# Gated mix of linear attention and a GEGLU MLP on one core: x blocks by position, wide sums and splits, phi into a zeroed tile, key sums by group

## The chip, the cores and the metric

The kernel runs on one core of a Trainium2 chip. The metric is device time in microseconds (us) of one execution, and of several executions the median. Beside those, one execution was taken with the hardware profiler; all rows of the profile and the trace come from that one.

The engines by their names in the profile: PE is TensorE's matmul, PEld its weight load, DVE is VectorE, ACT is ScalarE, POOL is GpSimd, SP is SyncE. In this kernel SP and POOL compute nothing: they issue DMAs. A "q" behind an engine's name stands for its sequencer.

## The reference

With S = 2048 tokens, D = 1024, H = 32 heads of 32 and a hidden width of 3584:

```python
g = sigmoid((x * gate_w).sum(-1, keepdims=True))
a = A(x, wqkv, w_phi, wo)          # linear attention
b = B(x, w_gate, w_up, w_down)     # (gelu(x @ w_gate) * (x @ w_up)) @ w_down
return g * a + (1 - g) * b

# A:
q, k, v = split(x @ wqkv)          # 32 heads of 32
pq, pk = q @ w_phi, k @ w_phi      # per head
phi_q = concat([softmax(pq), softmax(-pq)])      # 64 features, the same for phi_k
kv = phi_k^T @ v;  z = phi_k.sum(over tokens)
o = (phi_q @ kv) / (phi_q @ z + 1e-6)
a = o @ wo
```

Everything is float32.

## The kernel before

**Products.** Each large product is a block scheme with seven products in place of eight (Strassen's): x is cut into 2 x 2 blocks by token half and feature half (positions 11, 12, 21, 22), and four sums of these blocks, with three plain blocks, are the operands `x10, s1, s2, x11, s3, s4, x01`. For float32 accuracy each operand is split in two float32r parts, an upper one that ScalarE makes by a copy (`high`, L56) and a lower one that VectorE makes by a subtraction (`low`, L59). A product of 4 chunks of 128 is 12 matmuls of 128x512: upper by upper, upper by lower, lower by upper (`PASSES`), so the weights' lower half is asked for first by the third matmul.

**Units.** The work before the output part is a list of units: 8 of values (`v`), 8 of keys (`k`), then for each token half query units (`q`) and 28 gate and up units (`g`, `u`). A unit is seven slots of 12 matmuls on TensorE (L768); a slot takes some 2.72 us. `weights(n, ...)` loads a unit's weight block in even and odd part (`e`, `o` in "stage" tiles), splits e as `x`, forms sums of e and o (`quarter_sums`, `more_sums`), and splits these as `y` and `z` in tiles of the tag "tyz" (three buffers, `slot()`). `results(n, ...)` takes the products out of PSUM: L786, L800, L815 and L817 are ScalarE's copies between banks (the banks are a, b, c, c11, p), L781 is VectorE's subtraction of two products into a tile of the tag "h" (`hidden()`, three buffers).

**Order.** The order on TensorE, VectorE, ScalarE and SP is written at build time. Work that belongs to no fixed place is a Python generator (a "stream"): each `yield lo, hi, d, a` says from which slot on it may go, by which slot it must, and its costs on VectorE and ScalarE in us. `run_slot` takes streams that fit in the slot, by an estimate of both engines' clocks, and those that are due. Every engine then runs its list strictly in order: an instruction that waits holds all behind it.

**The start.** Values need x itself as weights and wv as moving data. `raws[i]` is a tile with the four positions of chunk pair i (three in "tyz" buffers, the fourth in three "h" buffers and one "qx"). A loop over the 8 chunks splits what has come and runs 12 matmuls each; `w_steps` makes the four sums in place, one chunk of 512 columns at a time (`sum_steps`), spread over this loop and units 1 and 2 by the table `extra`. `sums_high` and `sums_low` split them, 512 columns at a time. `phi_c` is loaded by one DMA and multiplied with a block mask into `bps`, the block diagonal weights with which `fold_piece` and others fold w_phi into wk and wq (L304, L447).

**Value stores.** `split_values` (L164 to L168) splits a result and stores it to DRAM in tensor `vt`, through buffers given by `value_homes` in turn: one "qx" buffer and three quarters of a work tile (`gated`).

**Features.** For each key half, group of four heads (8 groups) and 512 tokens there is a job (32 in all): max and min, exponentials, sums, scaled features f; f is added by an accumulating POOL DMA to `z_sum[g]` in DRAM (L985); then f is split and multiplied with the values (L1001), and `finish_kv` adds the result to `kz`. Jobs of key half 1 come first, then those of half 0, group by group.

**finish_z and attention.** After all of these, `finish_z` loads the eight `z_sum[g]` of 128x1024 in turn, reduces each over tokens (L1058), brings the sums into order, stores them in `z_rows` and spreads them by eight POOL DMAs into `kz` (L1081). `attention` then runs 32 jobs: `front` loads a query block (L1087), transposes it (L1106) and subtracts max and min; then come exponentials (L1138), the denominator with the sums z that `load_sums` has brought (L1092), the scaling, a transpose, the split (`pts`), and four matmuls (`attend`, L1205) whose results are stored for the output part. The output part (L1468) follows the last unit.

Of the kernel before, what the change touches and what calls it, by code (L numbers as in the profile page):

```python
# [16 lines left out]
P = 128  # L17
# [16 lines left out]
def tile_gated_mix(ctx: ExitStack, tc: tile.TileContext, x, xT, wkT, wqT, wv, w_phi, wo,  # L34
# [151 lines left out]
    with tc.manual_schedule(engines={PE, DVE, ACT, SP}):  # L186
# [5 lines left out]
        mask = fp.tile([P, 4, 32], F32, tag="st", name="mask", bufs=1)  # L192
        nc.vector.memset(mask, 0.0)
        for j in range(4):
            nc.vector.memset(mask[32 * j:32 * j + 32, j, :], 1.0)

        x_ops = {}
        raws = []
        for i in range(4):
            if i < 3:  # L200
                t = mid.tile([P, 4, BLK], F32, tag="tyz", name="raw", bufs=3)
                raws.append([t[:, n] for n in range(4)])
            else:
                raws.append([hidden() for _ in range(3)] + [fp.tile([P, BLK], F32, tag="qx", name="raw", bufs=1)])
# [13 lines left out]
        phi_c = fa.tile([P, NG, 32], F32, tag="o2", name="phi_c", bufs=1)  # L218
        nc.gpsimd.dma_start(phi_c, w_phi.rearrange("(g h) d f -> (h d) g f", h=4))
# [25 lines left out]
        x_sums = [w_steps(*raws[i]) for i in range(4)]  # L245
        ready = []

        steps_done = [0] * 4

        def sum_steps(n, upto=4):  # L250
            while n:
                left = [i for i in ready if steps_done[i] < upto]
                if not left:
                    break
                i = min(left, key=lambda i: (i > 0 and steps_done[i], i))
                next(x_sums[i])
                steps_done[i] += 1
                n -= 1

        bps = []  # L260
        for s in range(KC):
# [13 lines left out]
            if s >= 2:  # L275
                sum_steps(1)
            if s % 2:
                ready.append(i)
            if s == 3:
                both = fp.tile([P, 2, 4, 4, 32], F32, tag="vs", name="bp", bufs=1)  # L280
                for h in range(2):
                    t = both[:, h]
                    nc.vector.tensor_tensor(t, phi_c[:, 4 * h:4 * h + 4].unsqueeze(2).to_broadcast([P, 4, 4, 32]),
                                            mask.unsqueeze(1).to_broadcast([P, 4, 4, 32]), OP.mult)
                    bps.append(t)
# [30 lines left out]
        def sum_parts(k, kc):  # L316
            src, dst = raws[kc][SUM_AT[k]], [t[:, kc] for t in x_ops[0, (1, 2, 4, 5)[k]]]
            return (lambda: high(dst[0], src)), (lambda: low(dst[1], src, dst[0]))
# [17 lines left out]
        def sums_high(k, *kcs):  # L336
            if x_ops[0, (1, 2, 4, 5)[k]][0] is None:
                x_ops[0, 5] = [x_part(5, part) for part in range(2)]
            for kc in kcs:
                sum_parts(k, kc)[0]()  # L340

        def sums_low(k, *kcs):
            for kc in kcs:
                sum_parts(k, kc)[1]()
# [244 lines left out]
        def weights(n, half, kind, m):  # L589
# [14 lines left out]
            else:  # L604
# [24 lines left out]
                if fresh:  # L629
# [7 lines left out]
                    yield now[0] + 1, t, 1.25  # L637
# [224 lines left out]
        sums_at, folding, finishing, bank_free = [0], [2 * NG], [2 * NG + 1], [True]  # L862
# [64 lines left out]
        odd_even, others = rim[:, :2], rim[:, 8:40].rearrange("p (a b) -> p a b", a=2)  # L927
        blocks = lambda t: t.rearrange("p s (a b) -> p s a b", b=32)
# [5 lines left out]
        def features(jobs):  # L934
# [24 lines left out]
            while job:  # L959
# [25 lines left out]
                nc.gpsimd.dma_start(z_sum[g], wide[1], **({} if first else dict(accum_op=OP.add)))  # L985
                quiet = now[0] + 2
# [59 lines left out]

        def finish_z():
            while not free[0]:
                yield now[0] + 1, NEVER, 0.0
            both_z = xa.tile([P, 2, 1024], F32, tag="pts", name="zs", bufs=1)  # L1050
            rows = [both_z[:, i] for i in range(2)]
            for g in range(2):
                nc.sync.dma_start(rows[g], z_sum[g])
            yield now[0] + 2, NEVER, 0.0
            many = wide[1][:, :32 * NG].rearrange("p (g n) -> p g n", g=NG)
            for g in range(NG):
                yield now[0], NEVER, 1.25
                nc.vector.tensor_reduce(many[:, g], rows[g % 2].rearrange("p (n r) -> p n r", r=32), AX.X, OP.add,  # L1058
                                        apply_transpose=True)
                if g + 2 < NG:  # L1060
                    nc.sync.dma_start(rows[g % 2], z_sum[g + 2])
                    if g % 2:
                        yield now[0] + 2, NEVER, 0.0
            yield now[0], NEVER, 0.4
# [51 lines left out]
        def attention(jobs):  # L1116
# [6 lines left out]
            while job:  # L1123
# [16 lines left out]
                if key is not None:  # L1140
                    held[key] = False
# [368 lines left out]
```

## Time and profile before

| | |
|---|---|
| Time, median of 3 runs | 2343.64 us (2341.89 to 2345.09) |
| Profiled execution, its own time | 2341.32 us |
| Span of its instructions | 2339.5 us |
| TensorE granted clock | 1.000 |
| PE busy | 2314.3 us, 99% of the span, 10414 matmuls |
| VectorE busy | 1745.1 us, 75% |
| ScalarE busy | 1212.6 us, 52% |
| POOL busy | 388.7 us, 17% |
| DMA | 645.97 MB, mean 276 GB/s |
| Units | from about 27 us to 1648 us; then the output part |

How to read it: the profile gives for every instruction its start and duration, and from the semaphores what released it. A row of a timeline is start us, duration us, engine, line, operation, tile written<-tiles read, shape, count; in brackets the idle time of the engine just before, and what ended it. A row of the list of waits is who waited, for whom, then total us, times, longest us. An instruction's duration on VectorE overlaps the next one's start a little, so what one costs in a row of such is the distance of starts.

### The profile page before, as it was taken

The numbers are of one execution on the slowest core, as the hardware profiler recorded it, in microseconds if no ns is written. First come the engines' busy times: TensorE is split into PE (matmuls) and PEld (weight loads), VectorE is DVE, ScalarE is ACT, GpSimd is POOL, SyncE is SP. The second block draws the span as 40 slices with busy tenths as digits, with TensorE's granted clock in tenths as the row PEclk, the third lists the DMA queues.
The fourth block names the chain that finished last, engine by engine and source line by source line (L and its number), as shares of the span: only waits on it lengthen the run. The fifth ranks groups of instructions, "written<-read, shape, count | busy, mean of one in ns | idle before, by whom it ended". The sixth has DMA issues, their size and how long they took to land. (4 is left out here: it accounts for less than half of the span.)

```text
span 2339.5 us, 29686 instructions
## 1 busy us (share of the span) xinstructions
PE 2314.3 (99%) x10414; PEld 1916.1 (82%) x10414; DVE 1745.1 (75%) x2394; ACT 1212.6 (52%) x1703; POOL 388.7 (17%) x618
## 2 busy tenths in 40 slices
PE   9999999999999999999999999999999999999999
PEld 7788888888888888877888777878788888888887
DVE  8667557888888878756878788887674868867874
ACT  6445456565656555545777677777533322323321
POOL 2443332222222222211111111111000000000000
PEclk9999999999999999999999999999999999999999
DMA  7889988888889999997878877877874867977873
GB/s 234 272 300 336 325 286 343 292 313 298 303 305 302 310 301 306 299 320 278 271 246 269 255 246 237 263 244 235 289 276 153 288 233 251 342 260 270 294 263 135
DMA packets 263894, 645.97 MB, mean 276 GB/s; under 512 B 32048, under 2 KB 68416, under 8 KB 255808
## 3 DMA queue, kind: packets, MB, share of 16 engines
q1 hardware_dynamic: 204736, 428.67, 55.0%
q0 software_dynamic: 58736, 215.27, 26.4%
q8 instruction: 82, 1.34, 0.2%
q14 instruction: 68, 0.56, 0.1%
q10 hardware_dynamic: 272, 0.13, 0.0%
HBM read 429.00 MB, written 215.23 MB: 275 GB/s over the span
## 5 line engine op out<-in xcount | busy, mean ns | idle before, releaser
L1468 PE MATMUL po<-tw,wgu 128*128 128x512 f32 x1344 | 309.8, 389 | 0.0
L56 ACT ACTIVATE wgu<-stage 128x1024 fp32r<-128x1024 f32 (+2 forms) x166 | 172.6, 1040 | 257.7 <-DVE stage L1358 164.7
L1468 PEld LDWEIGHTS po<-tw,wgu 128*128 128x128 f32 x1344 | 252.3, 188 | 52.4
L59 DVE TENSOR_TENSOR wgu<-stage,wgu 128x1024 fp32r<-128x1024 f32 (+2 forms) x135 | 161.6, 1197 | 85.9 <-ACT wgu L56 84.8
L768 PE MATMUL p<-s1h,tyz 128*128 128x512 f32 x624 | 205.7, 391 | 4.9 <-DVE tyz L59 3.2
L768 PE MATMUL a<-s2h,tyz 128*128 128x512 f32 x624 | 205.6, 390 | 3.5 <-DVE tyz L59 2.5
L768 PE MATMUL c<-x01h,tyz 128*128 128x512 f32 x624 | 206.1, 391 | 2.8 <-ACT c L800 2.7
L768 PE MATMUL a<-x10h,wgu 128*128 128x512 f32 x624 | 205.6, 390 | 2.6 <-DVE h L781 2.6
L768 PE MATMUL a<-s4h,v 128*128 128x512 f32 x632 | 207.7, 389 | 0.0
L768 PE MATMUL b<-s3h,tyz 128*128 128x512 f32 x624 | 205.5, 390 | 0.0
L768 PE MATMUL c<-x11h,wgu 128*128 128x512 f32 x624 | 205.0, 389 | 0.0
L1468 PE MATMUL po<-tyz,wgu 128*128 128x512 f32 x672 | 155.7, 389 | 1.2 <-DVE wgu L59 0.7
L1468 PE MATMUL po<-tw,wl 128*128 128x512 f32 x672 | 156.9, 389 | 0.0
L1468 PEld LDWEIGHTS po<-tyz,wgu 128*128 128x128 f32 x672 | 126.0, 188 | 28.2 <-DVE wgu L59 1.2
L1468 PEld LDWEIGHTS po<-tw,wl 128*128 128x128 f32 x672 | 126.1, 188 | 26.2
L768 PEld LDWEIGHTS p<-s1h,tyz 128*128 128x128 f32 x624 | 116.8, 188 | 31.8 <-DVE tyz L59 4.9
L768 PEld LDWEIGHTS a<-s2h,tyz 128*128 128x128 f32 x624 | 117.0, 188 | 29.1 <-DVE tyz L59 3.3
L768 PEld LDWEIGHTS c<-x01h,tyz 128*128 128x128 f32 x624 | 117.2, 188 | 28.0 <-ACT c L800 4.2
L768 PEld LDWEIGHTS a<-x10h,wgu 128*128 128x128 f32 x624 | 117.2, 188 | 27.6 <-DVE h L781 3.5
L768 PEld LDWEIGHTS a<-s4h,v 128*128 128x128 f32 x632 | 118.6, 188 | 24.5
L768 PEld LDWEIGHTS b<-s3h,tyz 128*128 128x128 f32 x624 | 117.2, 188 | 24.3 <-ACT b L817 0.4
L768 PEld LDWEIGHTS c<-x11h,wgu 128*128 128x128 f32 x624 | 117.1, 188 | 24.3
(458 smaller groups left out, 4874.5 us busy)
## 6 DMA issues: line engine op xcount, KB each, us to landing
stage<-lm SPq DMA_DIRECT2D x98, 512.0 KB, 4.4
sr<-in_w_down SPq DMA_DIRECT2D x84, 512.0 KB, 4.9
sl<-lm SPq DMA_DIRECT2D x70, 512.0 KB, 4.7
lm<-h POOLq DMA_DIRECT2D x112, 256.0 KB, 5.1
stage<-in_w_gate SPq DMA_DIRECT2D x42, 512.0 KB, 4.4
stage<-in_w_up SPq DMA_DIRECT2D x42, 512.0 KB, 6.3
vs<-vt SPq DMA_DIRECT2D x32, 512.0 KB, 4.2
zs<-w POOLq DMA_DIRECT2D x32, 512.0 KB, 6.0
```

The source lines that it names most:

```text
L56: nc.scalar.activation(dst, src, AF.Copy)
L59: nc.vector.tensor_tensor(dst, src, dst_h.bitcast(F32), OP.subtract)
L768: nc.tensor.matmul(dst, w[:, h, kc, :], xq[e][:, kc, :], start=first and kc == 0 and i == 0, stop=kc == 3 and i == 2, skip_group_check=True)
L1468: nc.tensor.matmul(ps[c], lefts[s][:, a, m, c * P:(c + 1) * P], made[k][:, e, m], start=d == 0 and m == 0 and n == 0, stop=d == n_duo - 1 ...
```

## The change

Matmuls stay as many as they were, with the same operands. In the order of the code:

- `mask`, `phi_c` and the two products with the mask are gone. `phi_wide` (128x1024) is set to zero, and four POOL DMAs put w_phi's four heads of each group in their places.
- `whole[0..3]` are four tiles, one for each position, with all four chunk pairs in them: three "tyz" buffers and the lower half of operand s4's tile. `w_steps` runs on two chunks at once (two generators `x_sums[0]`, `x_sums[1]`, 1024 columns), and so do `sums_high` and `sums_low`. The table `extra` and the loop place them anew; one step and two pairs of splits stay for unit 2.
- One `plain_out` (ScalarE's copy of a value result) is moved from unit 1's first slot to before it.
- In `weights`, y's lower half may go in the same slot as `more_sums` and is due one slot earlier, in units 2, 3 and 9 (`soon`).
- `value_homes` has six buffers in turn: two of the "h" tag are added.
- Key sums: a stream `z_part(g)` starts when the last store of a group's features has been issued (for the last group, the last but one), and five slots later loads `z_sum[g]` in two halves of 128x512 on SP, reduces each, and keeps 8 numbers a partition in `quarters()`. The last job's features are not stored but reduced in place. `finish_z` adds the two and goes on as before.
- `attention` loads the sums z not before it starts, but after the first job's exponentials and not before `sums_at` (six slots after `finish_z`), then waits two slots.
- `attend` runs its four matmuls with the upper half for both p first, then the lower half.

```diff
-        mask = fp.tile([P, 4, 32], F32, tag="st", name="mask", bufs=1)
...
+        phi_wide = fp.tile([P, 2, 4, 4, 32], F32, tag="vs", name="bp", bufs=1)
+        nc.vector.memset(phi_wide, 0.0)
+        bps = [phi_wide[:, h] for h in range(2)]
...
+        whole = [mid.tile([P, 4, BLK], F32, tag="tyz", name="raw", bufs=3) for _ in range(3)]
+        whole.append(x_part(5, 1, F32))
+        raws = [[t[:, i] for t in whole] for i in range(4)]
...
-        nc.gpsimd.dma_start(phi_c, w_phi.rearrange("(g h) d f -> (h d) g f", h=4))
+        for j in range(4):
+            rows = slice(32 * j, 32 * j + 32)
+            nc.gpsimd.dma_start(phi_wide[rows].rearrange("p h g j f -> p (h g) j f")[:, :, j],
+                                w_phi.rearrange("(g j) d f -> j d g f", j=4)[j])
...
-        x_sums = [w_steps(*raws[i]) for i in range(4)]
+        x_sums = [w_steps(*[t[:, 2 * q:2 * q + 2] for t in whole]) for q in range(2)]
...
-            if s >= 2:
-                sum_steps(1)
...
+            if s in (3, 5, 7):
+                next(x_sums[0])
...
-        sums_high(0, 0, 1, 2)
+        sums_high(0, 0)
         quarter_sums(first_e, first_o, True)
         first_high("y", first_o)
-        sums_low(0, 0, 1, 2)
-        sum_steps(100, 1)
-        sums_high(0, 3)
+        sums_low(0, 0)
+        plain_out(0, 1, 0)
+        next(x_sums[1])
+        sums_high(0, 1)
         first_low("y", first_o)
-        sums_low(0, 3)
+        sums_low(0, 1)
...
-                    yield now[0] + 1, t, 1.25
+                    soon = n < 4 or n - 1 == TURNS[0]
+                    yield now[0] + (not soon), t - soon, 1.25
                     low(yl, o, yh)
...
                 yield lambda: fp.tile([P, BLK], F32R, tag="qx", name="vh", bufs=1)
-                for t in (gated(0, 0), gated(0, 1), gated(1, 0)):
-                    yield lambda t=t: t.bitcast(F32R)
+                yield lambda: fa.tile([P, BLK], F32R, tag="h", name="vh", bufs=3)
+                yield lambda: gated(0, 0).bitcast(F32R)
+                yield lambda: gated(0, 1).bitcast(F32R)
+                yield lambda: fa.tile([P, BLK], F32R, tag="h", name="vh", bufs=3)
+                yield lambda: gated(1, 0).bitcast(F32R)
...
-                nc.gpsimd.dma_start(z_sum[g], wide[1], **({} if first else dict(accum_op=OP.add)))
-                quiet = now[0] + 2
+                if job != (0, NG - 1, 1):
+                    nc.gpsimd.dma_start(z_sum[g], wide[1], **({} if first else dict(accum_op=OP.add)))
+                    quiet = now[0] + 2
+                    if half == 0 and j == (g < NG - 1):
+                        start(z_part(g))
+                else:
+                    yield now[0], NEVER, 1.25
+                    nc.vector.tensor_reduce(last_rows, wide[1].rearrange("p (n r) -> p n r", r=32), AX.X, OP.add,
+                                            apply_transpose=True)
...
+        def z_part(g):
+            yield now[0] + 5, NEVER, 0.0
+            for i in range(2):
+                nc.sync.dma_start(work[:, 0], z_sum[g][:, BLK * i:BLK * i + BLK])
+                yield now[0] + 3, NEVER, 0.65 + 0.1 * i
+                nc.vector.tensor_reduce(z_rows_of[:, 16 * i:16 * i + 16], work[:, 0].rearrange("p (n r) -> p n r", r=32),
+                                        AX.X, OP.add, apply_transpose=True)
+            nc.vector.tensor_reduce(quarters()[:, g], z_rows_of.rearrange("p (n t h) -> p n h t", n=2, t=4), AX.X, OP.add)
+            finishing[0] -= 1
...
-            yield sums_at[0], NEVER, 0.0
-            load_sums(job[1])
...
+                if "z" not in shared:
+                    yield max(now[0], sums_at[0]), NEVER, 0.0
+                    load_sums(g)
+                    yield now[0] + 2, NEVER, 0.0
...
-                    for p in range(2):
-                        for q in range(2):
+                    for q in range(2):
+                        for p in range(2):
                             nc.tensor.matmul(po[p], kbs[:, p].rearrange("p i a b -> p (i a b)"), pts[:, q, p, :],
...
         extra = {
...
+            1: {1: [*folds[:2], (lambda: more_sums(first_e, first_o, True), 1.4), (lambda: first_high("z", first_e), 0.0, 1.05),
+                    step(1), step(1), (lambda: first_low("z", first_e), 1.2),
+                    outs[1], (lambda: sums_high(1, 0, 1), 0.0, 2.1), (lambda: sums_low(1, 0, 1), 2.44)],
+                2: [*folds[2:4], (lambda: sums_high(2, 0, 1), 0.0, 2.1), (lambda: sums_low(2, 0, 1), 2.44), step(0)],
                 4: [*folds[4:], outs[2], outs[3]]},
+            2: {2: [step(1), (lambda: sums_high(3, 0), 0.0, 1.05)],
+                3: [(lambda: sums_low(3, 0), 1.22), (lambda: sums_high(3, 1), 0.0, 1.05), (lambda: sums_low(3, 1), 1.22), *puts[:1]],
+                5: puts[1:2]},
```

More of the change, by code (lines that the diff above doesn't have):

```diff
@@ L243, in weight_part @@
             return (lambda: high(dst[0], src)), (lambda: low(dst[1], src, dst[0]))
-        x_sums = [w_steps(*raws[i]) for i in range(4)]
[L246 to L260, printed above, removed]
+        x_sums = [w_steps(*[t[:, 2 * q:2 * q + 2] for t in whole]) for q in range(2)]
         for s in range(KC):
@@ L274, in tile_gated_mix @@
             w_low()
-            if s >= 2:
-                sum_steps(1)
[L277 to L285, printed above, removed]
+            if s in (3, 5, 7):
+                next(x_sums[0])
             for n, (a, e) in enumerate(PASSES):
@@ L314, in tile_gated_mix, with sum_parts @@
         SUM_AT = (3, 0, 2, 1)
-        def sum_parts(k, kc):
-            src, dst = raws[kc][SUM_AT[k]], [t[:, kc] for t in x_ops[0, (1, 2, 4, 5)[k]]]
+        def sum_parts(k, q):
+            src, *dst = [t[:, 2 * q:2 * q + 2] for t in (whole[SUM_AT[k]], *x_ops[0, (1, 2, 4, 5)[k]])]
             return (lambda: high(dst[0], src)), (lambda: low(dst[1], src, dst[0]))
@@ L927, in tile_gated_mix, with quarters @@
         odd_even, others = rim[:, :2], rim[:, 8:40].rearrange("p (a b) -> p a b", a=2)
+        z_rows_of = rim[:, 8:40]
+        last_rows = extremes.rearrange("p a b -> p (a b)")
+        def quarters():
+            if "zq" not in shared:
+                shared["zq"] = fp.tile([P, NG, 2, 4], F32, tag="kz", name="zq", bufs=1)
+            return shared["zq"]
         blocks = lambda t: t.rearrange("p s (a b) -> p s a b", b=32)
@@ L1045, in finish_kv @@
             finishing[0] -= 1
-        def finish_z():
[L1048 to L1064, printed above, removed]
-            nc.vector.tensor_reduce(wide[0][:, :64].rearrange("p (g s h) -> p g s h", g=NG, s=2),
-                                    many.rearrange("p g (s t h) -> p g s h t", s=2, t=4), AX.X, OP.add)
+        def z_part(g):
[7 more added lines that the diff above has]
+            finishing[0] -= 1
@@ L1067, in finish_z @@
+        def finish_z():
+            yield now[0], NEVER, 0.3
+            nc.vector.tensor_reduce(z_rows_of[:, :8].rearrange("p (n h) -> p n h", n=2),
+                                    last_rows.rearrange("p (n t h) -> p n h t", n=2, t=4), AX.X, OP.add)
+            eighth = quarters()[:, NG - 1]
+            nc.vector.tensor_tensor(eighth, eighth, z_rows_of[:, :8].rearrange("p (n h) -> p n h", n=2), OP.add)
             yield now[0], NEVER, 1.5
-            quarters, four = wide[0][:, :64], wide[0][:32, 256:512].rearrange("p (a q) -> p a q", q=4)
+            four = wide[0][:32, 256:512].rearrange("p (a q) -> p a q", q=4)
+            rows = quarters().rearrange("p g n h -> p (g n h)")
@@ L1069, in finish_z @@
             one, turned = wide[0][:32, 64:128], wide[0][:32, 128:192]
             for q in range(4):
-                nc.vector.tensor_copy(four[:, :, q], quarters[32 * q:32 * q + 32])
+                nc.vector.tensor_copy(four[:, :, q], rows[32 * q:32 * q + 32])
             nc.vector.tensor_reduce(one, four, AX.X, OP.add)
```

36 lines of the change are left out of this document (9 added, 27 removed).

## The prediction

> **What bounds the kernel now.** I read the busy times and the span with its granted clock first, then the list of waits of TensorE alone, then the timeline of each engine around the longest of these waits.
>
> ```profile
> PE 2314.3 (99%) x10414; PEld 1916.1 (82%) x10414; DVE 1745.1 (75%) x2394; ACT 1212.6 (52%) x1703; POOL 388.7 (17%) x618
> ```
> ```profile
> core 0: 2339.5 us, clock 1.000
> ```
>
> TensorE is busy 2314.3 of 2339.5 us and its granted clock never falls, so the matmuls themselves set the time. The change leaves their number as it is. What it can win is the 25.2 us in which TensorE stands still; what it can lose is any new stop. In the list of TensorE's waits (released by, total us, times, longest) these matter:
>
> ```profile
> PE misc L1205 <- DVE pts L59: 3.8, 5, 0.8
> PE p L768 <- DVE tyz L59: 3.2, 3, 1.3
> PE c L768 <- ACT c L800: 2.7, 1, 2.7
> PE a L768 <- DVE h L781: 2.6, 1, 2.6
> PE a L768 <- DVE tyz L59: 2.5, 2, 1.9
> ...
> PE a L768 <- ACT c L815: 1.0, 1, 1.0
> ...
> PE b L768 <- ACT b L817: 0.2, 1, 0.2
> ```
>
> The 13 rows of that list, of which the first and the last are shown, add up to 21.2 us; the seven shown are 16.0. Each can be placed in time, and each is touched by one part of the change.
>
> **Part 1, x blocks by position: sums and splits two chunks wide.** VectorE runs one instruction after another without a pause here; the starts give what one costs:
>
> ```profile
> 23.73 0.68 DVE L149 TENSOR_TENSOR raw<-raw 128x512 f32<-128x512 f32 x1
> 24.33 1.21 DVE L59 TENSOR_TENSOR s4h<-stage,s4h 128x1024 fp32r<-128x1024 f32 x1
> 25.47 0.68 DVE L136 TENSOR_TENSOR stage<-stage 128x512 f32<-128x512 f32 x1
> ```
>
> 512 columns cost 0.60 us from start to start, 1024 cost 1.14. Sixteen sums and sixteen lower halves become eight and eight: 32 x 0.60 - 16 x 1.14 = 1.0 us less. The two products with the mask go too, 2 x 0.6 = 1.2 us (512 columns each). So VectorE is about 2 us further when the second unit begins. TensorE does not wait for it before that, so this alone wins only the 0.2 us at ACT b L817; its use is in part 3.
>
> The bigger memset: before the first data VectorE stood idle for 3.17 us.
>
> ```profile
> 4.84 0.43 DVE L269 CAST w<-raw 128x512 fp32r<-128x512 f32 x1 [3.17 <-DMA raw<-in_wv]
> ```
>
> A memset of 1024 columns should take no longer than the subtraction of that width, 1.14 us, and it lies in that idle time: nothing. Phi now comes in four POOL issues instead of one, and POOL has room for three more at 0.91:
>
> ```profile
> 6.45 0.91 POOL L219 DMA_DIRECT2D phi_c<-in_w_phi  x1
> 31.84 0.57 POOL L307 DMA_DIRECT2D wk<-stage  x1 [24.48 <-ACT stage L56]
> ```
>
> The fourth is issued by about 10.1 us, and the first result made with phi leaves at 31.84: nothing, unless the cover of 20 us were gone.
>
> **Part 2, a slot that comes free later.** All three "tyz" buffers now hold x data. Positions 0 and 1 are needed until unit 2, slot 2, where the last wide sum stands on VectorE. The second of unit 2's weights ("z", due at slot 3) needs one of them, so ScalarE's split of z waits for that sum, and everything behind it on ScalarE too. In the old run, at this place:
>
> ```profile
> 50.32 0.76 DVE L167 TENSOR_TENSOR w<-h,w 128x256 fp32r<-128x256 f32 x2 [0.22 <-ACT w L164]
> ...
> 55.22 1.22 DVE L59 TENSOR_TENSOR tyz<-stage,tyz 128x1024 fp32r<-128x1024 f32 x1
> ```
>
> The second row is z's lower half, whole at 56.4; TensorE had then waited 2.5 - 1.9 = 0.6 us, so it asked at 55.8, and asks at 54.5 once the stop of 1.3 us ahead of it goes (part 3). Between the rows stood six instructions of 512 columns. Now it is unit 1's v (0.60, from 51.0), then the wide sum (to 52.8), z's upper half on ScalarE (1.06, a row in part 3) and its lower half (1.14): whole at about 55.0. That is a wait of 0.5 us where 0.6 stands now. I take no change, between 0.6 better and 1.5 worse.
>
> **Part 3, the early weights and six value homes.** y's lower half is now made one slot sooner in units 2, 3 and 9, directly behind the sums it needs. Unit 2:
>
> ```profile
> 45.67 1.06 ACT L56 ACTIVATE tyz<-stage 128x1024 fp32r<-128x1024 f32 x1 [1.38 <-issue]
> ```
> ```profile
> 48.89 1.21 DVE L59 TENSOR_TENSOR tyz<-stage,tyz 128x1024 fp32r<-128x1024 f32 x1
> ```
>
> The upper half is whole at 46.7, the lower one begins only at 48.9: on VectorE value splits and a subtraction stand between, which wait for ScalarE. Made at about 47, it ends 1.9 us sooner, and the longest of these waits of TensorE was 1.3. The same in units 3 and 9: all 3.2 us go (0 to 3.2 as bounds; the order is plain, so I take it whole).
> Unit 3's z was late for another reason: the four buffers for split values.
>
> ```profile
> 78.79 0.42 ACT L164 ACTIVATE w<-w 128x256 fp32r<-128x256 f32 x1 [1.96 <-DMA vt<-w]
> ```
> ```profile
> 80.32 1.22 DVE L59 TENSOR_TENSOR tyz<-stage,tyz 128x1024 fp32r<-128x1024 f32 x1
> ```
> ```profile
> L168 POOL DMA_DIRECT2D vt<-vh x16: 707/725/727, 48.0 to 185.9; - x16
> ...
>   ACT w L164: 11.8, 14
> ...
> DMA to landing us min/median/max: 2.4/5.1/8.0
> ```
>
> ScalarE waited 11.8 us in 14 places for stores of these buffers (the last view is that of the stores' line; the first row is one issue on POOL). Six buffers for the same eight uses a unit give each half as long again. The 1.9 us before unit 3's z go; bounds 0 and 1.9. Part 3: 5.1 us.
>
> **Part 4, key sums group by group.** The last job's store of sums falls away; VectorE reduces it in place (1.25 us, a row below). Now that store stands ahead of a query store on POOL:
>
> ```profile
> 1020.83 0.88 POOL L985 DMA_DIRECT2D zs<-w  x1 [5.44 <-DVE w L984]
> 1021.39 0.87 POOL L740 DMA_DIRECT2D q<-h  x1
> ```
> ```profile
> 1032.14 0.69 DVE L781 TENSOR_TENSOR h<-b,w 128x512 f32<-128x512 f32 x1 [4.50 <-DMA q<-h]
> ```
>
> VectorE stood 4.50 us for a buffer of that store, ScalarE's copy behind it came late, TensorE stood 2.7 us. If the query store lands 2.7 us sooner, all of it goes; bounds 0 and 2.7 (a loss is excluded, since a transfer falls away). I take 2.7, by the order of the two issues. The Trainium skill, "DMA: Bandwidth & Descriptors", section "Issuing engines are not separate DMA queues", says that all DMAs "will ultimately run on the same 16 DMA engines and interleave with each other"; by that, the reloads of the moment delay the query store as well, and the sum would be up to 2.7 us worse. No row here tells the two apart.
> Next, the load of the sums for attention:
>
> ```profile
> 1064.19 11.42 SPq L1092 DMA_DIRECT2D kz<-kz  x2
> ```
> ```profile
> 1078.58 0.71 DVE L1106 STREAM_TRANSPOSE stage<-qx 128x512 f32<-128x512 f32 x1 [9.95 <-DMA qx<-q]
> ```
>
> SP waited there until the sums were in place, and the next query load behind it came so late that VectorE stood 9.95 us in a transpose. Its whole chain then came at once, and TensorE waited 2.6 (DVE h L781) and 1.0 (ACT c L815). The load is now issued six slots after the sums were sent, about 16 us, against the 11.4 that SP waited; and the query block and its exponentials go ahead of it. I take 3.6 us; bounds 0 and 3.6.
> What is added: eight times two loads on SP and two reductions of 512 columns (half of 1.25 each) with a small one, put among the feature jobs; finish_z loses as many. The first load is issued five slots (13.6 us) after the last store of its group, whose landing (the store's line) took 9.9 us at worst, so SP is not held:
>
> ```profile
> DMA to landing us min/median/max: 3.0/6.0/9.9
> ```
>
> The second waits on SP for the first reduction, with reloads of weights behind it, and both reductions, three slots (8.2 us) after their loads, stand ahead of weight work on VectorE; a late load would hold that. The nearest row is finish_z itself:
>
> ```profile
> L1058 DVE TRANSPOSE_TENSOR_REDUCE w<-zs x8: 1245/1245/1246, 1036.4 to 1058.1; 128x32 f32<-128x1024 f32 x8
> ...
>   DMA zs<-zs: 15.3, 6
> ```
>
> VectorE stood 15.3 us in six such waits, and TensorE's list has no wait that came of them. I take 0.5 us of loss, between 0 and 3.
>
> **Part 5, attention's matmuls.** The two that need only the upper half now come first:
>
> ```profile
> 1326.78 0.96 PE L1205 MATMUL misc<-pts,kbs 128*128 128x512 f32 x3 [0.75 <-DVE pts L59]
> ```
> ```profile
> 1459.64 2.72 PE a L768 x12
> ```
>
> A matmul takes 2.72 / 12 = 0.23 us, so each of the five waits (3.8 us) shrinks by 0.23: 1.1 us. Attention also starts some 20 us sooner (the eight reductions, 1036.4 to 1058.1, are done before), so its steps meet the units elsewhere: between 2 better and 3 worse; I take 1.2 worse, as new waits can appear in more places than old ones stand.
>
> **The sum.** 0.2 + 0 + 5.1 + 2.7 + 3.6 - 0.5 + 1.1 - 1.2 = 11.0 us. The profiled execution took 2341.3 us (2339.5 of span and 1.8 around it), so 2330.3 by its measure. The median of the runs is 2343.6, 2.3 us above it, so I predict 2332.6. A change below 0.2% (4.7 us) can't be told from none.
>
> **Rivals.**
> First: the waits of parts 4 and 5 don't go but move. Feature jobs, sums and attention all shift, and VectorE is busy 75% of the time. For it: waits of 0.7 to 2.7 us lie scattered from 1015 to 1570. Against it: two have a cause that the change takes away by name. Then 5.3 (part 3 and the 0.2) and 1.1 remain, less 1.7 (the 0.5 and 1.2 above) to 4 (both losses nearer their worst ends): a gain of 2.4 to 4.7, 2339 to 2341.
> Second: the query store is held by the traffic and not by the store ahead of it. Then 2.7 us stay: 2335.3.
> Third, slower: two of the three "h" buffers become value homes, and the subtractions at L781 need one as well. A home is held for its split on ScalarE (0.42) and VectorE (half of 0.76), the issue (0.72) and the landing (5.1, at worst 8.0): 6.6 to 9.5 us. In the order of allocation a buffer comes round again after four slots at the closest, 4 x 2.72 = 10.9 us. If the hold passes that, VectorE stands as it did at 1032.14 and TensorE loses up to 2.7 us. There are 14 such subtractions in the value units; at 2 us each that is 28 us, and with the gains 2332.6 + 28 = 2361; from 8 of them on (16 us) the kernel is slower. Against it: 9.5 is below 10.9.
> Fourth: ScalarE's wait for the freed slot (part 2) is longer than I reckon, by up to 2.7 us, a slot: 2335.
>
> **Chances.** The forecast, with the fourth rival in it: 0.60, from 2327 to 2336. The second rival 0.12. The first 0.20, as it lies across the edge of 0.2% with 0.08 beyond it, 0.11 within and 0.01 slower. The third 0.06. More than forecast, towards all 21 us: 0.02. Faster by over 0.2%: 0.59 + 0.12 + 0.08 + 0.02 = 0.81; within: 0.01 + 0.11 = 0.12; slower: 0.07. The range 2327 to 2341 leaves out the third rival, the upper edge of the first and what lies below.
>
> **What would show it.** In the list of waits: no "p <- tyz" row of three times, "a <- tyz" down to one of about 0.6 us, no 2.7 for c, no 2.6 for h at L781. ScalarE's waits for value stores (now 11.8 us) below 4. No SP issue of kz over 3 us. L1205 waits near 0.5 each. The end of the unit loop earlier by 11 us, with the output part unchanged. The prediction is wrong if TensorE waits for L781 between 40 and 200 us (third rival), if z in unit 2 costs over 1.5 us, or if new waits of over 3 us in all stand among the feature jobs.

## The result, and the profile after

The changed kernel takes 2325.8 us (median of 6 runs, 2324.7 to 2328.2), the kernel before 2345.2 us in the same comparison (2341.9 to 2348.1): ratio 0.9918, 95% interval 0.9905 to 0.9931. Forecast were 2332.6 us and a range from 2327 to 2341, so the sign was right, and the gain larger than the range allowed, by 1.2 us. In the two profiled executions the span falls from 2339.5 to 2323.2 us, by 16.3 us where the sum of the prediction had 11.0. The largest part of it, 7.6 us, comes from a term for which a loss was forecast.

The busy times and the span of the changed kernel, then the list of TensorE's waits (released by, total us, times, longest):

```profile
PE 2310.4 (99%) x10414; PEld 1918.5 (83%) x10414; DVE 1746.4 (75%) x2390; ACT 1206.0 (52%) x1691; POOL 389.4 (17%) x620
core 0: 2323.2 us, clock 0.999
```
```profile
PE misc L995 <- DVE pts L59: 3.2, 1, 3.2
PE p L747 <- ACT w L765: 1.4, 2, 1.0
PE c L747 <- ACT c L779: 1.2, 2, 1.0
PE misc L1198 <- DVE pts L59: 1.2, 3, 0.5
PE misc L191 <- DVE ones L188: 1.1, 1, 1.1
PE a L747 <- DVE tyz L59: 0.5, 1, 0.5
PE b L747 <- ACT b L796: 0.3, 1, 0.3
PE a L747 <- ACT tyz L56: 0.2, 1, 0.2
```

(The line numbers have moved: L747, L779, L796, L995 and L1198 are the old L768, L800, L817, L1001 and L1205.) Gone are the three waits of "p" on VectorE, the 2.7 us of "c", the 2.6 us on "h"; attention's row fell from 3.8 us in 5 places to 1.2 in 3. The list adds up to 9.1 us where it was 21.2. The row at its head is new: 3.2 us in the matmuls of the feature jobs.

Where in time the gain comes from is seen by taking the start of the same product of the units in both traces and subtracting:

```
stretch (us, after)     before minus after     forecast
first product to 365    +6.8                   0.2 + 0 + 5.1
about 1011              -4.5                   -0.5
1022 to 1035            +3.0                   +2.7
1040 to 1105            +3.4                   +3.6
1110 to 1655            +7.6                   +1.1 - 1.2
rest of output part     0                      0
sum                     16.3                   11.0
```

(Between 1040 and 1105 us the changed kernel also does one attention step more, 4 matmuls or 0.9 us, which the row below gets back. The output part begins at 1634 us in the changed kernel; 1.8 of the 7.6 us are won in its first 25 us.) Two terms are far off: the loss at 1011 us, and the attention stretch. Each stop also costs some 0.25 us more than the list has for it: the old wait of 1.13 us on "p" at 50 us moved the next starts by 1.29 + 0.11 us. (The prediction took 1.3 us for that wait; this is the longest of the three on "p", which stood at 199 us.)

The new stop, in VectorE's, ScalarE's and TensorE's timeline of the changed kernel (start, us, what; in brackets the idle time before and what ended it):

```profile
1007.06 0.69 DVE L59 TENSOR_TENSOR s4l<-w,s4h 128x512 fp32r<-128x512 f32 x1 [5.96 <-ACT s4h L56]
1007.67 0.71 DVE L1046 TRANSPOSE_TENSOR_REDUCE rim<-w 128x16 f32<-128x512 f32 x1
1008.41 0.21 DVE L1048 TENSOR_REDUCE zq<-rim 128x8 f32<-128x32 f32 x1
1008.53 0.67 DVE L956 TENSOR_REDUCE extremes<-kx 128x16 f32<-128x512 f32 x1
1009.13 0.67 DVE L957 TENSOR_REDUCE extremes<-kx 128x16 f32<-128x512 f32 x1
1009.72 1.21 DVE L59 TENSOR_TENSOR pts<-w,pts 128x1024 fp32r<-128x1024 f32 x1
```
```profile
1006.39 0.63 ACT L56 ACTIVATE s4h<-w 128x512 fp32r<-128x512 f32 x1 [5.39 <-DMA w<-xs]
1006.93 1.04 ACT L56 ACTIVATE pts<-w 128x1024 fp32r<-128x1024 f32 x1
```
```profile
1011.08 1.19 PE L995 MATMUL misc<-pts,vs 128*128 128x256 f32 x8 [3.15 <-DVE pts L59]
```
```profile
1012.60:1016.00 3.40, 3.40 (x10) 2.62 (x9) 2.47 (x3) 1.31 (x3) 0.00 (x0) 0.50 0.73 241
```

The last part of x for the coming turn was loaded late; ScalarE stood 5.39 us for it with the feature job's upper half (pts) behind it, VectorE then had the reductions of the key sums (L1046, L1048) and two of another feature job (L956, L957) ahead of the job's lower half, and TensorE stood 3.15 us. The last view is a stretch by engine (busy PE, PEld, DVE, ACT, POOL, then the granted clock): behind the stop the clock was 0.50 for 3.41 us, 8 matmuls took 0.2 us more each, another 1.6 us.

The same queue stood there in the kernel before, with the same late load: it took 10.4 us to land, ScalarE waited 3.72 us for it, and the lower half of pts ended at 1014.9, where TensorE stood only 0.3 us (at 1015.02). There was no room left, so whatever came on top went to TensorE in full:

```profile
1013.70 1.22 DVE L59 TENSOR_TENSOR pts<-w,pts 128x1024 fp32r<-128x1024 f32 x1
```
```profile
PE misc L1001 <- PE a L768: 0.3, 1, 0.3
```

What came on top shows against the run e1 below, which has the rest of the change but not these loads and reductions; there the lower half of pts ends 2.64 us sooner (1008.29 against 1010.93). In the changed kernel the load of the x part is issued 1.26 us later (995.22 against 993.96), behind the second load of a group's sums; it takes 11.2 us and not 10.6; and the reductions on VectorE take 0.86 us (1007.67 to 1008.53).

```profile
994.06 0.82 SPq L1044 DMA_DIRECT2D w<-zs  x1
995.22 0.33 SPq L535 DMA_DIRECT2D w<-xs  x1
```

### The profile page after: what moved, and what is told of

Its sections match the earlier page's. It is cut to its first block, busy times and chain, and to the rows that moved or that the text cites. A ratio compares the mean times of both kernels' runs of the same rounds, so it can differ in the third digit from the quotient of the medians.

```text
span 2323.2 us, 29698 instructions
## 1 busy us (share of the span) xinstructions
PE 2310.4 (99%) x10414; PEld 1918.5 (83%) x10414; DVE 1746.4 (75%) x2390; ACT 1206.0 (52%) x1691; POOL 389.4 (17%) x620
## 5 line engine op out<-in xcount | busy, mean ns | idle before, releaser
L56 ACT ACTIVATE wgu<-stage 128x1024 fp32r<-128x1024 f32 (+2 forms) x166 | 172.6, 1040 | 255.1 <-DVE stage L1352 159.0
L747 PE MATMUL a<-s4h,v 128*128 128x512 f32 x632 | 209.1, 392 | 0.0
L747 PE MATMUL c<-x01h,tyz 128*128 128x512 f32 x624 | 205.8, 391 | 1.2 <-ACT c L779 1.2
L747 PE MATMUL p<-s1h,tyz 128*128 128x512 f32 x624 | 205.0, 389 | 1.4 <-ACT w L765 1.4
L747 PE MATMUL a<-s2h,tyz 128*128 128x512 f32 x624 | 205.4, 390 | 0.7 <-DVE tyz L59 0.5
L747 PE MATMUL b<-s3h,tyz 128*128 128x512 f32 x624 | 205.6, 390 | 0.3 <-ACT b L796 0.3
L747 PE MATMUL a<-x10h,wgu 128*128 128x512 f32 x624 | 205.3, 390 | 0.0
L747 PE MATMUL c<-x11h,wgu 128*128 128x512 f32 x624 | 205.0, 389 | 0.0
L747 PEld LDWEIGHTS a<-s4h,v 128*128 128x128 f32 x632 | 119.3, 189 | 24.8
L747 PEld LDWEIGHTS p<-s1h,tyz 128*128 128x128 f32 x624 | 117.1, 188 | 26.7 <-ACT w L765 2.2
L747 PEld LDWEIGHTS c<-x01h,tyz 128*128 128x128 f32 x624 | 117.2, 188 | 25.9 <-ACT c L779 2.1
L747 PEld LDWEIGHTS a<-s2h,tyz 128*128 128x128 f32 x624 | 117.0, 188 | 25.7 <-DVE tyz L59 1.0
L747 PEld LDWEIGHTS b<-s3h,tyz 128*128 128x128 f32 x624 | 117.2, 188 | 24.6 <-ACT b L796 0.7
L747 PEld LDWEIGHTS c<-x11h,wgu 128*128 128x128 f32 x624 | 117.1, 188 | 24.3
L747 PEld LDWEIGHTS a<-x10h,wgu 128*128 128x128 f32 x624 | 117.1, 188 | 24.1
```

Of the source, the lines that this page charges most:

```text
L56: nc.scalar.activation(dst, src, AF.Copy)
L747: nc.tensor.matmul(dst, w[:, h, kc, :], xq[e][:, kc, :], start=first and kc == 0 and i == 0, stop=kc == 3 and i == 2, skip_group_check=True)
```

## Experiments

Each is the changed kernel with the edit shown, if nothing else is said. Ratios are to the kernel before in the same comparison, whose median was 2345.1 to 2346.3 us each time.

**Old sums (e1).** The old finish_z, the store of the last job's sums and no z_part.

```diff
-                        start(z_part(g))
...
+            for g in range(NG):
...
+                nc.vector.tensor_reduce(many[:, g], rows[g % 2].rearrange("p (n r) -> p n r", r=32), AX.X, OP.add,
+                                        apply_transpose=True)
```

> The changed kernel with the old summing of the key features: all eight groups are stored, and after the last job the eight groups are loaded and reduced one after the other; all else as changed. Theory 1 (the unforeseen 6 us between 1110 and 1650 us and 2 us at the output part come from attention starting some 20 to 30 us sooner): attention starts near 1060 us again; the stop of 3.15 us near 1011 us with its half clock goes (4.5 us won); the query store waits behind the store of sums again (3.0 lost), and some 6 to 8 us of attention's gain are lost: about 2330 us. Theory 2 (the order of attention's matmuls brings them): those 6 to 8 us stay, about 2324 us. Theory 3 (chance of where attention's steps meet the units): anything from 2322 to 2332 us, with waits of TensorE at other places than in either kernel.

Measured: 2334.8 us, ratio 0.9951 (0.9938 to 0.9965). The stop at 1011 us goes (0.36 us left), the wait of "c" on the query store comes back (2.5 us at 1026), attention begins at 1091 us where the changed kernel has 1067, and a new stop of 4.0 us stands at 1062. From 1110 to 1650 us it loses 6.9 us against the changed kernel; 1.8 of these are two attention steps that it still has to do, so 5.0 us are lost. Theory 1 and theory 3 allow that and theory 2 does not. The time lies above all three forecasts, by the stop at 1062 with the half clock behind it, which none of them had.

**Attention's order of matmuls, undone (e2) and alone in the kernel before (e3).**

```diff
-                    for q in range(2):
-                        for p in range(2):
+                    for p in range(2):
+                        for q in range(2):
```

> The changed kernel with attention's four matmuls in the old order (both halves of one bank, then of the other). Theory 1 (earlier attention): only the 0.23 us at each wait on a lower half is lost, some 3 to 5 places, 1 us: 2326.8 us. Theory 2 (the order): about 6 us are lost, 2332 us, and the row of attention's matmuls waiting on a lower half goes from 1.2 us back to 3.8 or more.

Measured: 2326.2 us, ratio 0.9922 (0.9908 to 0.9936) against 0.9918 for the changed kernel; attention's row is 2.1 us in 4 places where it was 1.2 in 3.

> The kernel before with only the new order of attention's matmuls. Theory 1 (earlier attention): a gain of 5 x 0.23 = 1.1 us, 2344 us against 2345.2. Theory 2 (the order): a gain of about 6 us, 2339 us.

Measured: 2344.7 us, ratio 0.9995 (0.9987 to 1.0004); the row on the lower half is 2.7 us where it was 3.8. In these rows the order is worth about 1 us both ways. The times differ by 0.4 and 1.4 us, too little to be told from none. The 6 us of theory 2 are excluded; theory 2 falls.

**Attention 8 slots later (e4), and 14 (e7).**

```diff
-                elif not fjobs and not finishing[0] and jobs and now[0] >= jobs[0][0]:
+                elif not fjobs and not finishing[0] and jobs and now[0] >= max(jobs[0][0], sums_at[0] + 2):
```

(+ 8 in the second; sums_at is set 6 slots after the last instruction on the sums.)

> The changed kernel, but attention may start only 8 slots (22 us) after the last instruction on the key sums, near where it starts in the kernel before; nothing else is different. Theory 1 (earlier attention): the end of attention meets the output part again and its chain meets more of the last units, 4 to 8 us lost, about 2331 us. Theory 2 (the order): no change, 2326 us. Theory 3 (chance of the meeting places): waits at new places, 2322 to 2332 us, and the gain not tied to the end of attention.

Measured: 2330.7 us, ratio 0.9940 (0.9928 to 0.9952). From nothing but the later start some 5 us are lost. In the trace the loss stands between 1290 and 1390 us (5.9 us), not at the end; TensorE's rows for attention in this run:

```profile
PE misc L1198 <- DVE pts L59: 2.4, 5, 0.6
PE misc L1198 <- ACT pts L56: 1.7, 2, 0.9
```

> The changed kernel, but attention may start only 14 slots (38 us) after the last instruction on the key sums, 16 us later than in the run with 8 slots. Theory 1 (the later attention starts, the more it costs): worse than the run with 8 slots (ratio 0.9940), 2334 us or more, with a wait where the output part begins. Theory 3 (only the place of its steps against the units' work counts, not how late it is): between 2325 and 2331 us, better than the run with 8 slots or equal.

Measured: 2333.0 us, ratio 0.9944 (0.9931 to 0.9956), by which it can't be told from e4; it lies between what the two theories gave. So lateness does not add up: 8 slots cost all of it, 6 more nothing that can be measured. By the starts of attention's matmuls (see below) e7 loses 3.7 us in them where e4 loses 6.7. The only loss tied to the end is small. The first row is of this run, the others are of the kernel before:

```profile
PE po L1462 <- ACT h L1187: 0.7, 1, 0.7
```
```profile
PE po L1468 <- DVE wgu L59: 0.7, 1, 0.7
PE po L1468 <- ACT wgu L56: 0.5, 1, 0.5
```

TensorE waits where the output part begins, and in both the last attention step stands in slot 558. In e1 and e4 it stands in slot 555, in the changed kernel in 549, and there is no such wait.

That leaves the place of the steps. Counting the units' products in twelves gives every attention step the slot behind which its four matmuls stand. The planner works in slots, so e1 and e4, which begin differently, have all steps in the same slots from 395 on, and both lose between 1290 and 1400 us. Sorted by the place in the unit (slot modulo 7) and the slots since the step before, the 32 steps of eleven profiles (before, after, e1 to e5, e7, e8, e11, e12) give this; late means that a step's starts took over 0.12 us more than its matmuls need:

```
place in unit, slots since the step before    late, of    excess of a late one (us)
1, 5                                          11 of 11    0.55 to 2.65
2, 5                                           6 of 6     0.94 to 1.19
4, 7                                          15 of 17    0.32 to 1.23
3, 6                                          12 of 46    0.29 to 0.97
6, 5                                           8 of 43    0.17 to 3.60 (the longest with a half clock)
2, 6                                           5 of 31    0.20 to 0.42
1, 6 or more                                   0 of 85
all others (the first steps left out)          1 of 102   0.17
```

The kernel before has one step of the first kind (1.98 us), one of the second (1.19), two of the third (1.23, 1.03) and a bad one of the fifth (1.71); with the small ones 7.8 us. The changed kernel has one of the first (0.83), one of the third (0.47) and one of the fourth (0.71): 2.0 us. The difference of 5.8, and the 1.8 us that the two waits at the output part cost, are 7.6 us; TensorE's other stops after 1110 us are 0.9 us more than before, and the step done earlier gives 0.9: 7.6.

Why these are late is to be seen at one of them in the changed kernel, VectorE above, TensorE below:

```profile
1386.96 1.25 DVE L1181 STREAM_TRANSPOSE w<-w 128x1024 f32<-128x1024 f32 x1
1388.13 0.65 DVE L760 TENSOR_TENSOR h<-b,w 128x512 f32<-128x512 f32 x1
1388.82 0.69 DVE L707 TENSOR_TENSOR h<-h,w 128x512 f32<-128x512 f32 x1
1390.40 1.23 DVE L59 TENSOR_TENSOR pts<-w,pts 128x1024 fp32r<-128x1024 f32 x1 [0.88 <-ACT pts L56]
```
```profile
1390.50 0.65 PE L1198 MATMUL misc<-pts,kbs 128*128 128x512 f32 x2
1391.68 0.73 PE L1198 MATMUL misc<-pts,kbs 128*128 128x512 f32 x2 [0.53 <-DVE pts L59]
```

The unit's own subtractions (L760, L707) and ScalarE's evacuation stand between the transpose and the split of pts, so the lower half ends at 1391.6, behind the slot in which the plan put the matmuls. In the code the step is released by start(push()) without the time at which its lower half is planned to end; push then reads the beginning of the slot, and the matmuls are put into the next slot whatever VectorE still has to do. The experiments e6, e9 and e10 are on that; the one between is on the stop at 1011 us.

**No stop at 1011 (e5).**

```diff
-                if j == 3 and raw[3] is raw[0]:
-                    yield now[0] + 3, need - 2, 0.0
+                    yield now[0] + 5, need - 2, 0.0
```

> The changed kernel, but the split of the one x part that is loaded last (s4 of the turn at 995 us, loaded behind the second load of a group's sums) is put on ScalarE five slots after its load and not three; TensorE's order of matmuls is the same. Theory A (the new stop near 1011 us is the feature job's upper and lower halves queued behind that split, which waits 5.39 us for its load): the stop of 3.15 us falls below 0.5, the half clock behind it (8 matmuls at 0.2 us more, 1.6 us) goes, the rest is unchanged: 4.5 us less than the changed kernel, 2321.3 us. Rival (the feature job itself is late by the two reductions of the sums, 0.9 us, and by the earlier arrival of TensorE): at least 2 us of the stop stay, 2324 us or more.

Measured: 2322.6 us, ratio 0.9903 (0.9890 to 0.9917), 3.2 us below the changed kernel's median; TensorE's matmuls stand in the same order. The stop is

```profile
1008.48 1.19 PE L995 MATMUL misc<-pts,vs 128*128 128x256 f32 x8 [0.75 <-DVE pts L59]
```

and the clock never falls there. At 1026 us it is 4.2 us ahead; 0.9 is given back at 1044 us, where "c" now waits 1.1. Theory A holds, though 0.75 us of the stop stay where it said below 0.5. What stays is the load of the group's sums, for which VectorE now stands itself, and the reductions behind it:

```profile
1005.06 0.71 DVE L1046 TRANSPOSE_TENSOR_REDUCE rim<-w 128x16 f32<-128x512 f32 x1 [3.97 <-DMA w<-zs]
```

**Attention's matmuls released by the end of their lower half (e6, with the edit of e5).**

```diff
-                    fillers.append((passed[0], attend, 4, range(1, 7)))
+                    fillers.append((passed[0] + 1.0, attend, 4, range(1, 7)))
...
-                    start(push())
+                    start(push(), passed[0])
```

> The kernel of the run without the stop, and attention's matmuls are released by the planned end of the lower half they read plus 1 us, not in the next slot whatever VectorE does. If the waits on lower halves are what attention costs, the rows of attention's matmuls (1.2 us in 3 places) go to below 0.5 and the time falls by 1 us to 2320 us; if the place of attention's steps among the units decides, the release one slot later moves the steps behind it and waits come up elsewhere: 2320 to 2328 us.

Measured: 2319.3 us (2319.2 to 2319.4), ratio 0.9887 (0.9872 to 0.9902); 3.3 us less than e5 in the same comparison, more than expected. Not all of it is the edit's: in the two profiled executions the difference is 2.9 us, and 0.9 of it is there by 1200 us, up to where TensorE's matmuls stand in the same order in both; 2.1 us arise behind. Attention's row falls to 0.4 us in one place, and "c" on ScalarE's L779 is the largest left:

```profile
PE c L747 <- ACT c L779: 3.3, 3, 1.8
PE misc L1198 <- DVE pts L59: 0.4, 1, 0.4
```

**The late start with that release (e9).** The edits of e4, e5 and e6 together.

> Attention 8 slots late as in the earlier run, with the late split of s4 (no stop at 1011 us) and with attention's matmuls released by the planned end of their lower half plus 1 us. If the late start costs through matmuls that the plan places before their lower half is done (in slots 1 or 2 of a unit five slots behind the last step, or slot 4 seven behind it), the release takes that away: TensorE's waits in attention's matmuls (2.4 and 1.7 us in the late run) fall below 1 us together and the time is within 3 us of the early run with both edits, 2319 to 2322 us. If lateness itself costs (busier units, the output part), 5 us or more stay: 2324 us or more.

Measured: 2318.9 us, ratio 0.9889 (0.9876 to 0.9903): the same as the early start. Attention's row, against the two of e4 above:

```profile
PE misc L1198 <- DVE pts L59: 1.0, 3, 0.4
```

Its profiled execution took 2323.6 us: against e6 it lost 3.8 us in the first 70 us, at unit 2's z and by a half clock, and from 1105 us on it was 0.3 us better. So with this release the start eight slots later costs nothing that can be measured, where it cost 5 us without; theory 1 falls.

The release also changes the places of the steps. In the profiles of e6, e9 and e10 only one step of 93 is of the first three kinds of the table, and it is not late; eight are late, by 0.2 to 1.0 us, six of them at place 3, six slots behind the last.

**The release in the kernel before (e10).** The edit of e6 there, without that of e5.

> The kernel before with one edit: attention's matmuls released by the planned end of their lower half plus 1 us. If its waits in attention (6.4 us of gaps ahead of these matmuls) come from matmuls placed too early, some 5 us are won: 2340 us against 2345. If they come from where attention's chain meets the units, they move to other engines and products: 2343 to 2347 us.

Measured: 2338.4 us, ratio 0.9964 (0.9954 to 0.9974), some 8 us won by the medians. Between the two profiled executions it is 4.1 us, where e10 had two half clocks and the kernel before none. Its profile has 1.6 us in 3 places for attention instead of 3.8 in 5 and 1.0 in 2, and no wait where the output part begins; "c" on ScalarE grew from 2.7 us to 4.8 in 3 places, one of 2.05 us in the last unit. The ratio is 0.36% below 1 where the whole change's is 0.82%: four tenths of its gain can be had with two lines at the planner.

**Four value homes (e8).**

```diff
-                yield lambda: fa.tile([P, BLK], F32R, tag="h", name="vh", bufs=3)
```

(twice, in value_homes.)

> The changed kernel with four value homes and not six. By the prediction's step (the 1.9 us before unit 3's z, and its wait of 11.8 us on ScalarE for value stores): 1.9 us are lost near 80 us, 2327.7 us, and ScalarE waits some 10 us for value stores again. Rival (x laid by position and the earlier lower halves alone had made room): nothing lost in the first 220 us. Third: what is done early in the first units moves the attention part too; then the end differs by more than the loss at 220 us.

Measured: 2332.5 us, ratio 0.9944 (0.9931 to 0.9956). At 220 us it is 6.9 us behind the changed kernel and at the end 7.5. ScalarE waits for stores again,

```profile
ACT w L164 <- DMA vt<-w: 13.3, 11, 3.4
```

and unit 3's z costs 0.5 + 2.2 us of standing at 79 to 82 us, with a half clock of 1.5 us behind it: 4.2 us. Another 2 us are in the first 60 us, where runs differ by as much among themselves (unit 2's z waited 1.35 us on ScalarE here, 1.42 in e9, which has six homes, 0.17 in the changed kernel's profile). The prediction's step holds in kind, and at twice the size or more; the rival, nothing lost, falls. The third reading falls too, since the loss at 220 us and at the end differ by only 0.6 us.

**The old place of y's lower half (e11).**

```diff
-                    yield now[0] + (not soon), t - soon, 1.25
+                    yield now[0] + 1, t, 1.25
```

> The changed kernel with y's lower half one slot later again in units 2, 3 and 9 (undone: the early place). By the prediction's step: 3.2 us lost before 220 us, as three waits of the first y product, with the rest unchanged: 2329 us. Rival (the six value homes had brought VectorE and ScalarE so far ahead that the old place would do): less than 1.5 us lost, 2327 us or less.

Measured: 2326.9 us, ratio 0.9920 (0.9908 to 0.9933), the same as the changed kernel. One wait comes back, 0.9 us at 195 us (unit 9); in units 2 and 3 none does. The rival holds.

**The old place of the first load of sums (e12).**

```diff
+            yield sums_at[0], NEVER, 0.0
+            load_sums(job[1])
             e, f = blocks(e2), blocks(f2)
```

> The changed kernel with the load of the first key sums ahead of attention's loop again, where SP waits for the sums with the next query load behind it; the sums group by group stay. By the prediction's step: the waits of 2.6 and 1.0 us between 1060 and 1100 us come back, 3.6 us, 2329.4 us, with an SP issue of the sums over 8 us. Rival (the sums are there in time since they are added up group by group, so that the place of the load costs nothing): no new wait before 1110 us, and only the place of attention's steps changes, 2324 to 2330 us.

Measured: 2332.2 us, ratio 0.9944 (0.9931 to 0.9956). SP holds

```profile
1038.71 6.80 SPq L1083 DMA_DIRECT2D kz<-kz  x2
```

(the changed kernel 4.17 us at 1039.82) and between 1050 and 1105 us nothing is lost against the changed kernel: the two waits do not come back. The rival holds up to there. The loss, 7.8 us at the end of the profile (6.4 by the medians), arises between 1110 and 1250 us: the second and third step moved to slots 370 and 379, a later one is then of the second kind (slot 401), steps in the same slots as in the changed kernel run late, and the largest stop, 3.0 us of "c", hangs on a store of attention's results that holds an "h" buffer:

```profile
1234.76 0.69 DVE L760 TENSOR_TENSOR h<-b,w 128x512 f32<-128x512 f32 x1 [6.17 <-DMA la<-h]
```

In the changed kernel the same instruction waits 2.57 us there. What made the store that much later was not tried.

## Why the prediction was right and wrong, step by step

- **Part 1 and 2** (0.2 and nothing): right in the changed kernel's profile. Unit 2's z waits 0.5 us on its lower half, as reckoned, and 0.2 on ScalarE, within the bounds. In the profiles of e8 and e9 the same z cost 1.9 us, over the 1.5 that the prediction gave as a sign of being wrong, so the fourth rival is real in some executions. The memset and the phi issues cost nothing that the traces show.
- **Part 3** (5.1): some 6 us (6.3 by 214 us with part 1, 6.8 by 365), but divided wrongly. The value homes were put at 1.9 us and are worth the 2.7 us of waits that e8 brings back, plus a half clock there (by the times e8 is some 6 us slower than the changed kernel); y's early lower half was put at 3.2 and is worth about 1 (e11), as with the homes and the wide sums in place units 2 and 3 did without it. ScalarE's waits for value stores, 11.8 us, are gone from its list.
- **Part 4, query store** (2.7): right, 3.0 us. The second rival, with its rule of the Trainium skill ("DMA: Bandwidth & Descriptors", "Issuing engines are not separate DMA queues"), is not borne out here in what was drawn from it, that the traffic alone would hold the query store: with the store ahead of it gone the wait goes, and with that store back (e1) it returns at 2.5 us. But a wait for a query store stands a few slots later now and was not there before; it costs TensorE 0.2 us in the changed kernel and 1.1 in e5:

```profile
1046.34 0.69 DVE L760 TENSOR_TENSOR h<-b,w 128x512 f32<-128x512 f32 x1 [5.71 <-DMA q<-h]
```
- **Part 4, load of the sums** (3.6): 3.4 us were won in that stretch (4.3 with the attention step done earlier), but e12 shows that the place of the load did not bring them. That the sums are ready earlier is what is left; no run changes that alone (e1, where they are late again, loses 7 us between 1040 and 1068 us, by another wait and its half clock). The late place of the load is worth some 6 us further on, by the times of e12, where attention's steps fall otherwise. The sign "no SP issue of kz over 3 us" did not come true: one takes 4.17.
- **Part 4, what is added** (-0.5, bounds 0 to 3): mis-sized, -4.5. The prediction named the danger (a late load ahead of weight work on VectorE) and priced it by finish_z, whose 15.3 us of waits on VectorE had cost TensorE nothing. But there nothing that TensorE soon needed stood behind them; here the feature job's pts did, and these had no room left even before (0.3 us of standing). It also left out that a stop can halve the clock.
- **Part 5, the order** (1.1): about 1 us in the rows of waits of e2 and e3, as reckoned; the times can't tell it.
- **Part 5, the re-timing of attention** (taken as -1.2, bounds 2 better to 3 worse): this step failed. Attention's matmuls were 5.8 us better off (about 1 of it from the order), and the output part 1.8. The prediction read attention's waits as five small ones, to be shortened by 0.23 us each, with new ones as likely as old ones. Beside the row that it quoted, the profile had a second one for the same steps:

```profile
PE misc L1205 <- ACT pts L56: 1.0, 2, 0.7
```

and the excess of starts at all of them was 7.8 us. The bound on the better side should have been that much, as nothing fixed the steps to their slots. The gain itself is luck: the change did not aim at these places, and a start 8 or 14 slots later (e4, e7) or the old place of the load (e12) is 5 to 7 us slower. Without that row the profile would have gained 8.7 us, less than the forecast 11.0.
- **The rivals.** The third (value homes as "h" buffers make TensorE wait at L781 between 40 and 200 us) did not come: the list of after has no such row. The first (the waits move) was half true: one of 3.2 us came, among the feature jobs; new waits of over 3 us there were one of the prediction's own signs of being wrong.
- **The measure.** The profiled execution of before stood 2.3 us below the median then known, and the prediction added these 2.3 us to the changed kernel's time too. There the profiled execution stood only 0.7 us below the median (2325.1 to 2325.8). So of the 6.8 us between 2332.6 and 2325.8 the traces show 5.2, and 1.6 come from this sum; they are more than the 1.2 us by which the range was missed.

## What to carry to other kernels

When a change moves a long chain of small steps that is slotted by hand between other work, read for each step whether its operand was done in the slot where its consumer stands, before and in the new place; the sum of these excesses in the old place, not the few waits that a list shows, bounds what re-timing can win there. A release that does not carry the end of its producer is a fault of the plan: mending it made a start eight slots later cost nothing (e9 against e6, where e4 against the changed kernel lost 5 us) and is the cheaper change. And price an added load by what stands behind its consumer in the queue at that moment, and by how much room that has, not by what the same load cost elsewhere.

## What was not expected of the hardware

The half clock does not follow the length of a stop. Stops of 2.1 and 2.2 us (e10, at 1033 and 1642 us, measured by the starts like those that follow) were followed by 3.41 us at clock 0.5; the stops of 2.9 and 2.7 us in the kernel before, of 3.4 us in e11 and of 3.0 and 3.2 us in e12 were not. It came 14 times in 9 of the 14 profiles, the end of the kernel left out, and cost some 1.5 to 1.7 us each time. The stretch at full clock ahead of each is a whole multiple of 3.413 us (10, 16, 22, 78, 177, 278, 295 and 301 of them among others), so the decision falls on a fixed grid, and where a stop lies on it is chance. What sorts the stops is how long TensorE stands within one window of that grid: all nine windows with over 1.95 us of standing were followed by a half clock, four of the six with 1.89 to 1.94, and of those with less only one (1.67 us, e9). The stops that passed were split between two windows or came close: the longest standing in one window was 1.74 us in the kernel before, 1.71 in e11 and 1.94 in e12. The Trainium skill, "TensorE: Matmul & The Clock Gate", section "What's actually happening", has a free-running window of 3413 ns, with which this agrees; by its table the clock falls after at least one idle window, where here about 2 us of standing in a window were enough.
